# Sigmoid attention and a two-layer MLP: splitting of q, k, v and of the weights moved from GpSimd to ScalarE and VectorE

## Chip, cores and metric

The kernel runs on 1 core of one Trainium2 chip. The metric is the device time of one execution in microseconds (us).

## The reference

```python
scores = scale * np.matmul(q, k.transpose(0, 1, 3, 2)) - np.log(S)   # q, k, v: (8, 12, 448, 64) f32
attn = 1.0 / (1.0 + np.exp(-scores))
x = (attn @ v).transpose(0, 2, 1, 3).reshape(B * S, H * D)           # 3584 x 768
h = x @ w_in                                                         # w_in 768 x 2048
g = np.where(h >= 1, h, np.where(h <= -1, 0.0, (h + 1) ** 2 / 4))
out = g @ w_out                                                      # w_out 2048 x 768
```

## The kernel before

**Precision by splitting.** TensorE multiplies f16, and the kernel keeps f32 precision by writing a scaled operand as two f16 halves: hi is the f16 rounding of s*w, and lo is s*w - hi. A product then takes three matmuls (hi hi, hi lo, lo hi). What the change touches is who computes hi and lo. s is a power of two that is found from the largest magnitude.

**Attention.** Two heads form a pair; there are 48 pairs, six to a batch. Pairs 0 to 7 are multiplied as f32 from tensors that come laid out for it. Pairs 8 to 13 have q and k split (two parts of 128x448), pairs 14 to 47 have q, k and v split (two parts of 128x448 and one of 128x512). `load_pair` (L247) loads a pair three pairs ahead, `prep_a` (L267) finds the magnitudes on VectorE two pairs ahead, and `prep_b` (L283) finds the scales and splits. Then eight small DMAs on SyncE's queue copy the halves from `hl` into `qk` (L312, L313), and `scores`, `weigh` and `av` do the two products and the sigmoid, a piece (`step`) at a time. The raw tile has two buffers, so that a pair's load waits for the split of the pair two before.

In `prep_b` GpSimd does three instructions for each part: it scales the raw part in place (L303), writes hi (L304) and subtracts to get lo (L305).

**Weights.** w_in and w_out come as f64 words and are turned into f32 in 16 chunks each of 128x768 (`Weight.convert`: ScalarE L178 and L202, VectorE L185, L186 and L189). w_in's loads are on SyncE's queue during batch 0, w_out's mostly on ScalarE's. Once the scale of a group of eight chunks is known (`find_scale`), `Weight.split` writes the halves. It has two forms. With `pool` GpSimd scales in place (L220), ScalarE writes hi (L221), GpSimd writes lo (L222). Without it ScalarE writes hi with the scale (L224), and VectorE writes lo in one instruction (L225). Chunk f's halves lie where the f32 of chunk f-1 lay, so that the splits follow each other. Chunks 0 to 3 of w_in are split without `pool` (chunk 2 twice), 4 to 15 with it. In w_out every second chunk goes to GpSimd.

**MLP.** x of a batch is split (`finish_x`: ScalarE L448, VectorE L449). `up` makes 18 matmuls for a chunk (L517) and then g: ScalarE L526, VectorE L527 and L528, ScalarE L529 (hi), VectorE L530 (lo). L528 is the last reader of the PSUM tile `ph`, of whose tag there are three. `down` makes the second product (L549).

**Order.** Batch 0 is attention alone, together with the conversion of w_in. After it the units of the MLP of batch b are interleaved with the pieces of attention of batch b+1, and in batch 0's MLP with the rest of w_in, the conversion of w_out and its splits. Tile's scheduler orders every engine's instructions from the program order with priorities. Each engine then works its own list in order.

Of the kernel before, what the change touches and what calls it, by code (L numbers as in the profile page):

```python
# [18 lines left out]
AF = mybir.ActivationFunctionType  # L19
ALU = mybir.AluOpType  # L20
# [14 lines left out]
NHALF = 6  # L35

NA = 8
AHEAD = 2
LAST = 92
LAST1 = 20  # L40
# [4 lines left out]
B0 = 3  # L45
B1 = 64
GPOOL = 1
POOL_FROM = 2
MAX_ACT = 7
L0 = 10  # L50
A0 = 17
# [6 lines left out]
def sigmoid_attention_mlp(ctx: ExitStack, tc: tile.TileContext, first_qvk, qkv, w_in, w_out, out_t):  # L58
    nc = tc.nc
# [8 lines left out]
    NPIECE = NP * NPC  # L68
    GROUPS = slice(0, NA), slice(NA, NFC)
    LAG = 3  # L70
# [23 lines left out]
    def scales(m, n, tag, pool=None, square=False):  # L94

        pool = pool or sml_p
        few = {"bufs": 2} if tag == "x" else {}
        mask, top = (EXP_MASK - EXP_ONE, TOP - 1) if square else (EXP_MASK, TOP)
        e = sml_p.tile([P, 3], F32, tag="e", name=tag + "_e")[:, :n]
        nc.vector.tensor_scalar(out=e, in0=m, scalar1=TINY, scalar2=None, op0=ALU.max)  # L100
        ei = e.bitcast(I32)
        nc.vector.tensor_scalar(out=ei, in0=ei, scalar1=mask, scalar2=None, op0=ALU.bitwise_and)
        s = pool.tile([P, n], F32, tag=tag + "_s", name=tag + "_s", **few)
        nc.vector.tensor_scalar(  # L104
            out=s.bitcast(I32), in0=ei, scalar1=-1.0, scalar2=float((2 * 127 + top) * EXP_ONE), op0=ALU.mult, op1=ALU.add
        )
        inv = pool.tile([P, n], F32, tag=tag + "_i", name=tag + "_i", **few)
        nc.vector.tensor_scalar(  # L108
            out=inv.bitcast(I32), in0=ei, scalar1=float(top * EXP_ONE), scalar2=None, op0=ALU.subtract
        )  # L110
        return s, inv
# [7 lines left out]
        out=ident, in_=ident, pattern=[[-1, P]], compare_op=ALU.is_equal, fill=0.0, base=0, channel_multiplier=1  # L119
# [19 lines left out]
    class Weight:  # L139
# [27 lines left out]
        def convert(self):  # L167

            f = self.at - 2
            if 0 <= f < NFC:  # L170
                if f + 1 not in (NA, NFC):
                    self.sum(f)
                if self is wo:
                    self.load(3 if f == 3 else 1)
            f = self.at
            if f < NFC:
                a = self.f32(f)
                nc.scalar.activation(a, self.words_of(f)[1].bitcast(F32), AF.Abs, scale=HIGH_SCALE)  # L178
            f = self.at - 1
            if 0 <= f < NFC:  # L180

                low, high = self.words_of(f)
                a = self.f32(f)
                ai = a.bitcast(I32)
                nc.vector.tensor_scalar(out=ai, in0=ai, scalar1=3, scalar2=None, op0=ALU.logical_shift_left)  # L185
                nc.vector.scalar_tensor_tensor(  # L186
                    out=ai, in0=low, scalar=29, in1=ai, op0=ALU.logical_shift_right, op1=ALU.bitwise_or
                )
                nc.vector.scalar_tensor_tensor(  # L189
                    out=ai, in0=high, scalar=-0x80000000, in1=ai, op0=ALU.bitwise_and, op1=ALU.bitwise_or  # L190
                )
                if f + 1 in (NA, NFC):
                    self.sum(f)
                if self is wi:
                    self.load(1, nc.sync)
            self.at += 1
# [18 lines left out]
        def split(self, f, pool=False):  # L215
            if f >= NFC:
                return
            w, hi, lo, scale = self.f32(f), self.sb[:, f, 0, :], self.sb[:, f, 1, :], self.scale[f >= NA]
            if pool:
# [22 lines left out]
    def first_time(what, p):  # L242
        new = (what, p) not in done
        done.add((what, p))
        return new
# [37 lines left out]
    def prep_b(p):  # L283
        if not NFULL <= p < NPAIR or not first_time("split", p):
            return
        r, m = raws.pop(p), maxes.pop(p)
        n = 2 if p < NFULL + NHALF else 3

        s, inv = scales(m, n, "qkv")
        sqk = sml_p.tile([P, 1], F32, tag="sqk", name="sqk")  # L290
        nc.vector.tensor_scalar(
            out=sqk, in0=inv[:, 0:1], scalar1=inv[:, 1:2], scalar2=1.0 / math.sqrt(D), op0=ALU.mult, op1=ALU.mult
        )
        hl = hls.pop(p, None) or stk_p.tile([P, 2, 2, S], F16, tag="hl", name="hl")
        parts = [hl[:, 0], hl[:, 1]]
        if n == 3:
            v = stk_p.tile([P, 2, VW], F16, tag="v", name="v", bufs=3)
            parts.append(v)
        else:
            v = ready[p]  # L300
        for t, dst in enumerate(parts):
            rt, hi = r[:, t * S : 2 * S + VW if t == 2 else (t + 1) * S], dst[:, 0, :]
            nc.gpsimd.tensor_scalar(out=rt, in0=rt, scalar1=s[:, t : t + 1], scalar2=1.0, op0=ALU.mult, op1=ALU.mult)  # L303
            nc.gpsimd.tensor_scalar(out=hi, in0=rt, scalar1=1.0, scalar2=1.0, op0=ALU.mult, op1=ALU.mult)  # L304
            nc.gpsimd.tensor_tensor(out=dst[:, 1, :], in0=rt, in1=hi, op=ALU.subtract)  # L305

        qk = stk_p.tile([P, 2, 2, S], F16, tag="qk", name="qk")
        for j in range(2):
            src = slice(j * D, (j + 1) * D)
            for h in range(2):  # L310
                dst = slice(h * D, (h + 1) * D)
                nc.sync.dma_start(out=qk[dst, j, 0], in_=hl[src, 0, 0, :])  # L312
                nc.sync.dma_start(out=qk[dst, j, 1], in_=hl[src, 1, h, :])  # L313
        ready[p] = qk, v, sqk, inv, hl
# [168 lines left out]
    def group_scales(b, inv_x, k):  # L483

        up_sc[b, k] = sc = up_scales(*largest(inv_x, k), k)
        down_sc[b, k] = lambda: small("od%d" % k, inverse("ig%d" % k, sc[4]), wo.inv[k], ALU.mult)
# [24 lines left out]
    def up(b, f, u):  # L511
# [9 lines left out]
        if u == NCC // 2 - 1:  # L521
            ihr, hr, rt, ihs, _ = up_sc[b, int(f >= NA)]
            g = tmp_p.tile([P, S], F32, tag="tmp", name="g")
# [69 lines left out]
    wi = Weight(w_in, w_in_sb, "wi", [5 + 2 * (f % 6) for f in range(NFC)])  # L593
    wo = Weight(w_out, w_out_sb, "wo", [13, 15, 9, 11, 13, 15, 9, 11, 0, 0, 13, 15, 0, 0, 0, 0])
# [9 lines left out]
    with tc.manual_schedule(engines={mybir.EngineType.SP}):  # L604
# [9 lines left out]
        while at < NPIECE:  # L614
            step(at)
            at += 1
            for what, when in ((load_pair, L0), (prep_a, A0), (prep_b, A0 + 1)):
                for k in range(2):
                    if at == when + LSTEP * k:
                        what(NFULL + k)  # L620
            convert(wi, min((NA + 1) * at // WI_A, NA + 1 + max(0, at - WI_A) * (NFC - NA) // (NPIECE - WI_A + WI_B)))
            if at == WI_A:
# [11 lines left out]
    for u, unit in enumerate(units):  # L634
        while at < 2 * NPIECE and B0 + (at - NPIECE) * (B1 - B0) // NPIECE <= u:
            step(at)
            at += 1
        if wi.at < NFC + 1:
            n = NPIECE - WI_A
            convert(wi, NA + 1 + min(NFC - NA, (n + u + 1) * (NFC - NA) // (n + WI_B)))  # L640
            if wi.at == NFC + 1:
                wi.find_scale()
                group_scales(0, inv_x, 1)
        f, r = divmod(u, NCC // 2)
        if r == 0 and f < NFC:
            wi.split(f + AHEAD, f >= POOL_FROM)
        if wo.at < NA + 1:
            convert(wo, min(NA + 1, (u + 1) * (NA + 1) // WO_A))
            if wo.at == NA + 1:
                wo.find_scale()  # L650
                split_at = 0
        elif wo.at < NFC + 1:
            convert(wo, min(NFC + 1, NA + 1 + (u + 1 - WO_A) * (NFC - NA) // (WO_B - WO_A)))
            if wo.at == NFC + 1:
                wo.find_scale()
                roots()
        if len(wo.scale):
            while split_at < min(NA, 2 * (u + 1 - WO_A)):
                wo.split(split_at, split_at % 2 == 1)
                split_at += 1  # L660
        unit()
    inv_x = finish_x(1)
    common_scales(1, inv_x)
    for b in range(1, B):
        units = ups(b) + downs(b)
        last = LAST
        if b == 1:
            units = ups(1, 0, NA) + downs(0, 1) + ups(1, NA, NFC) + downs(1)
            last = len(units) - LAST1
        first = at  # L670
        for u, unit in enumerate(units):
            while at < min(b + 2, B) * NPIECE and (at - first) * (last - 1) // NPIECE <= u:
                step(at)
                at += 1
            if b == 1:
                while split_at < min(NFC, NA + (u + 1) * (NFC - NA) // (NA * NCC // 2 - 2)):
                    wo.split(split_at, split_at % 2 == 1)
                    split_at += 1
            unit()
            if b + 1 < B and u == last:  # L680
                inv_x = finish_x(b + 1)
                common_scales(b + 1, inv_x)
# [39 lines left out]
```

## Time and profile before

| | |
|---|---|
| median of 3 runs | 1202.59 us (1200.89 to 1203.66) |
| the profiled execution | 1202.2 us |
| its span, from the first to the last instruction | 1200.5 us |
| TensorE busy | 1166.8 us (97%) |
| VectorE, ScalarE, GpSimd busy | 64%, 47%, 31% of the span |
| mean granted TensorE clock | 0.994 |

A row of the profile names line, engine, operation and tiles (PE is TensorE, PEld its weight loads, DVE is VectorE, ACT ScalarE, POOL GpSimd, SPq SyncE's queue), output before input. Busy time is the time of the instructions; idle time is put down to what ended it.

### The profile page before, as it was taken

Reading aid. Unit: us, or ns where it says so; the run is one execution under the profiler, and the core shown is the slowest. Engines: PE = TensorE matmul, PEld = TensorE weight load, DVE = VectorE, ACT = ScalarE, POOL = GpSimd, SP = SyncE. Lnnn points to the kernel's source line nnn. Section 1 sums busy time; section 2 is a strip of 40 time slices with the busy share of each in tenths; the row PEclk is TensorE's granted clock in tenths of the full one; section 3 lists DMA queues with packets and bytes.
Section 4 is the critical chain, followed back from the end, with each engine's and each line's share of the span. In section 5 each row is a group of like instructions: output and inputs, shape, how many; then the busy total and the mean of one; then the engine's idle time right before and its main releaser. Section 6 shows DMA issues by size and latency. Waiting matters only on the chain.

```text
span 1200.5 us, 16814 instructions
## 1 busy us (share of the span) xinstructions
PE 1166.8 (97%) x6366; PEld 556.6 (46%) x6366; DVE 770.7 (64%) x1440; ACT 566.1 (47%) x811; POOL 371.4 (31%) x458
## 2 busy tenths in 40 slices
PE   7989799899999999999999999999999999999998
PEld 2324343444445444444444444454444444445554
DVE  6879978673753686458854787448874688336510
ACT  6979546452531554336533464336543466323300
POOL 0362665633420342413252234223424223100000
PEclk9999899999999999999999999999999999999999
DMA  9855125213120122212122112221212220100000
GB/s 320 316 191 210 49 57 180 88 40 117 54 82 24 48 56 64 73 58 75 40 71 79 56 40 55 87 56 50 77 41 75 63 68 17 31 22 10 1 16 31
DMA packets 47985, 92.72 MB, mean 77 GB/s; under 512 B 7712, under 2 KB 36896, under 8 KB 47904
## 3 DMA queue, kind: packets, MB, share of 16 engines
q1 hardware_dynamic: 46176, 82.21, 22.3%
q10 hardware_dynamic: 1728, 9.44, 2.2%
q8 instruction: 50, 0.82, 0.3%
q14 instruction: 31, 0.25, 0.1%
HBM read 60.88 MB, written 12.39 MB: 61 GB/s over the span
## 4 chain that ended last, share of the span: by engine, by line
PE 72%; issue 9%; DVE 7%; POOL 6%; DMA 3%; ACT 3%; SPq 0%; POOLq 0%; ACTq 0%; DVEq 0%
PE po L549 30%; PE ph L517 27%; PE pav L423 7%; PE psc L338 3%; PE psc L347 2%; PE psc L331 2%; POOL hl L305 1%; DMA raw<-qkv 1%; POOL raw L303 1%; POOL hl L304 1%; DMA w_out_sb<-w_in 1%; DVE m L280 1%; PE psc L353 1%; DVE g L527 1%; DVE w_out_sb L186 1%
## 5 line engine op out<-in xcount | busy, mean ns | idle before, releaser
L517 PE MATMUL ph<-xhl,w_in_sb 128*128 128x448 f16 x2304 | 449.1, 354 | 10.7 <-DVE g L528 6.1
L549 PE MATMUL po<-ghl,w_out_sb 128*128 128x448 f16 x2304 | 445.0, 353 | 0.9 <-DVE w_out_sb L225 0.9
L517 PEld LDWEIGHTS <-w_in_sb 128*128 128x128 f16 x2304 | 222.1, 98 | 237.2 <-issue 38.1
L549 PEld LDWEIGHTS <-w_out_sb 128*128 128x128 f16 x2304 | 221.8, 98 | 218.9 <-issue 13.7
L303 POOL TENSOR_SCALAR raw<-raw,qkv_s 128x448 f32<-128x448 f32 (+1 forms) x114 | 81.7, 731 | 527.2 <-DVE qkv_i L108 526.9
L382 ACT ACTIVATE psc<-psc,nls,sqk 128x896 f32<-128x896 f32 (+1 forms) x136 | 128.1, 972 | 212.9 <-PE psc L347 204.6
L391 DVE SCALAR_TENSOR_TENSOR ahl<-psc,ahl 128x896 f16<-128x896 f32 (+1 forms) x170 | 151.2, 900 | 68.1 <-ACT ahl L390 66.8
L390 ACT ACTIVATE ahl<-psc 128x896 f16<-128x896 f32 (+1 forms) x170 | 124.2, 763 | 51.2 <-DVE ahl L391 50.9
L529 ACT ACTIVATE ghl<-g 128x448 f16<-128x448 f32 x128 | 73.7, 577 | 123.8 <-DVE g L528 123.6
L280 DVE TENSOR_REDUCE m<-raw 128x2 f32<-128x896 f32 x74 | 63.5, 897 | 97.3 <-DMA raw<-qkv 97.3
L526 ACT ACTIVATE g<-ph,hr,ihr 128x448 f32<-128x448 f32 x128 | 92.2, 721 | 62.7 <-PE ph L517 55.2
L527 DVE SCALAR_TENSOR_TENSOR g<-g,rk 128x448 f32<-128x448 f32 x112 | 96.1, 858 | 21.2 <-ACT g L526 19.0
L530 DVE TENSOR_TENSOR ghl<-g,ghl 128x448 f16<-128x448 f32 x128 | 87.8, 686 | 34.0 <-ACT ghl L529 32.3
L305 POOL TENSOR_TENSOR hl<-raw,hl 128x448 f16<-128x448 f32 x80 | 92.5, 1175 | 0.0
L559 DVE TENSOR_SCALAR o<-po,od 128x448 f32<-128x448 f32 x48 | 32.6, 682 | 93.1 <-PE po L549 83.4
L528 DVE SCALAR_TENSOR_TENSOR g<-ph,ihs,g 128x448 f32<-128x448 f32 x128 | 87.2, 682 | 3.3
L423 PE MATMUL pav<-ahl,v 128*64 128x448 f16 x748 | 84.6, 356 | 0.0
L338 PE MATMUL psc<-qk 128*128 128x448 f16 x252 | 63.4, 354 | 1.5 <-ACT a L379 1.5
L331 PE MATMUL psc<-ghl 128*128 128x448 f32 (+1 forms) x128 | 51.4, 583 | 11.0 <-DMA ghl<-first_qvk 5.9
L448 ACT ACTIVATE xhl<-x,x_s 128x448 f16<-128x448 f32 x48 | 27.7, 655 | 69.6 <-DVE x_s L104 69.6
L423 PEld LDWEIGHTS <-v 128*64 128x64 f16 x748 | 38.8, 109 | 32.8 <-issue 12.6
L304 POOL TENSOR_SCALAR hl<-raw 128x448 f16<-128x448 f32 x80 | 52.8, 674 | 0.0
(114 smaller groups left out, 820.3 us busy)
## 6 DMA issues: line engine op xcount, KB each, us to landing
raw<-qkv SPq DMA_DIRECT2D x34, 704.0 KB, 4.3
qk<-hl SPq DMA_DIRECT2D x320, 56.0 KB, 2.0
w_out_sb<-w_in SPq DMA_DIRECT2D x16, 768.0 KB, 9.5
out_t<-o SPq DMA_DIRECT2D x48, 224.0 KB, 2.0
w_out_sb<-w_out ACTq DMA_DIRECT2D x6, 768.0 KB, 5.0
raww<-w_out ACTq DMA_DIRECT2D x6, 768.0 KB, 6.0
ghl<-first_qvk SPq DMA_DIRECT2D x8, 448.0 KB, 7.5
w_out_sb<-w_out SPq DMA_DIRECT2D x4, 768.0 KB, 8.0
```

Of the source, the lines that this page charges most:

```text
L303: nc.gpsimd.tensor_scalar(out=rt, in0=rt, scalar1=s[:, t : t + 1], scalar2=1.0, op0=ALU.mult, op1=ALU.mult)
L305: nc.gpsimd.tensor_tensor(out=dst[:, 1, :], in0=rt, in1=hi, op=ALU.subtract)
L338: nc.tensor.matmul(out, kq[:, j, 1, w], kq[:, j, 0, :], start=True, stop=False)
L382: nc.scalar.activation(a, a, AF.Sigmoid, bias=nls, scale=sqk)
L390: nc.scalar.activation(hi, x, AF.Copy, scale=ATT)
L391: nc.vector.scalar_tensor_tensor(out=lo, in0=x, scalar=ATT, in1=hi, op0=ALU.mult, op1=ALU.subtract)
L423: nc.tensor.matmul(pav[j * D : (j + 1) * D, :S], *terms[j][t], start=c == 0 and t == 0, stop=mid and t == len(terms[j]) - 1,)
L517: nc.tensor.matmul(ph[:, :S], w_in_sb[:, f, wh, c * P : (c + 1) * P], xhl[:, c, xh, :], start=c == 0 and wh + xh == 0, stop=c == NCC - 1 a ...
L526: nc.scalar.activation(g, ph[:, :S], AF.Relu, bias=hr, scale=ihr)
L527: nc.vector.scalar_tensor_tensor(out=g, in0=g, scalar=rt, in1=g, op0=ALU.min, op1=ALU.mult)
L530: (nc.gpsimd if f % GPOOL else nc.vector).tensor_tensor(out=ghl[:, f, 1, :], in0=g, in1=hi, op=ALU.subtract)
L549: nc.tensor.matmul(po[:, :S], w_out_sb[:, f, wh, m * P : (m + 1) * P], ghl[:, f, gh, :], start=f == lo and wh + gh == 0, stop=f == hi - 1 ...
```

## The change

Pairs 8 to 17 are now split as the weights already could be: ScalarE writes hi with the scale, VectorE writes lo in one instruction from the raw part and hi. Pairs 18 to 47 stay on GpSimd. All 16 chunks of w_out are split by ScalarE and VectorE. In w_in the odd chunks from 3 on go to GpSimd, the even ones to ScalarE and VectorE; chunk 3 thus moves to GpSimd, chunks 4, 6, 8, 10, 12 and 14 away from it.

```diff
+QK_POOL = 18
-POOL_FROM = 2
...
-            nc.gpsimd.tensor_scalar(out=rt, in0=rt, scalar1=s[:, t : t + 1], scalar2=1.0, op0=ALU.mult, op1=ALU.mult)
-            nc.gpsimd.tensor_scalar(out=hi, in0=rt, scalar1=1.0, scalar2=1.0, op0=ALU.mult, op1=ALU.mult)
-            nc.gpsimd.tensor_tensor(out=dst[:, 1, :], in0=rt, in1=hi, op=ALU.subtract)
+            st = s[:, t : t + 1]
+            if p < QK_POOL:
+                nc.scalar.activation(hi, rt, AF.Copy, scale=st)
+                nc.vector.scalar_tensor_tensor(
+                    out=dst[:, 1, :], in0=rt, scalar=st, in1=hi, op0=ALU.mult, op1=ALU.subtract
+                )
+            else:
+                nc.gpsimd.tensor_scalar(out=rt, in0=rt, scalar1=st, scalar2=1.0, op0=ALU.mult, op1=ALU.mult)
+                nc.gpsimd.tensor_scalar(out=hi, in0=rt, scalar1=1.0, scalar2=1.0, op0=ALU.mult, op1=ALU.mult)
+                nc.gpsimd.tensor_tensor(out=dst[:, 1, :], in0=rt, in1=hi, op=ALU.subtract)
...
-            wi.split(f + AHEAD, f >= POOL_FROM)
+            wi.split(f + AHEAD, f % 2 == 1)
...
-                wo.split(split_at, split_at % 2 == 1)
+                wo.split(split_at)
...
-                    wo.split(split_at, split_at % 2 == 1)
+                    wo.split(split_at)
```

## Rows read from the trace of the kernel before

**Rows 1.** Page, part 1: busy us, share of the span, instructions.

```profile
PE 1166.8 (97%) x6366; PEld 556.6 (46%) x6366; DVE 770.7 (64%) x1440; ACT 566.1 (47%) x811; POOL 371.4 (31%) x458
```

**Rows 2.** Waits of TensorE: total us, times, longest.

```profile
PE ph L517 <- DVE g L528: 6.1, 4, 2.0
...
PE pm L127 <- DVE g L528: 4.5, 2, 4.2
PE ph L517 <- ACT xhl L448: 3.1, 1, 3.1
...
PE psc L338 <- ACT a L379: 1.5, 1, 1.5
...
PE po L549 <- DVE w_out_sb L225: 0.9, 1, 0.9
```

**Rows 3.** Waits from 55 to 75 us, TensorE's on the sigmoid.

```profile
PE psc L331 <- ACT a L379: 3.5, 2, 2.0
```

**Rows 4.** Four stages: PE, PEld, DVE, ACT, POOL busy; granted clock, DMA.

```profile
40.00:75.00 35.00, 31.52 (x113) 10.66 (x111) 31.61 (x49) 29.03 (x45) 24.84 (x18) 0.99 0.58 189
75.00:120.00 45.00, 43.49 (x204) 17.22 (x202) 41.55 (x80) 40.05 (x63) 13.65 (x10) 0.97 0.66 249
120.00:165.00 45.00, 34.99 (x178) 16.07 (x175) 39.68 (x62) 25.05 (x41) 29.72 (x24) 0.92 0.20 58
165.00:255.00 90.00, 84.21 (x422) 35.77 (x420) 68.02 (x139) 48.82 (x69) 45.79 (x40) 0.98 0.32 96
```

**Rows 5.** VectorE's groups from 40 to 255 us: busy us, mean ns, idle before.

```profile
L530 DVE TENSOR_TENSOR ghl<-g,ghl 128x448 f16<-128x448 f32 x21 | 18.4, 874 | 7.0 <-ACT ghl L529 6.8
L527 DVE SCALAR_TENSOR_TENSOR g<-g,ru 128x448 f32<-128x448 f32 x16 | 16.8, 1052 | 1.2 <-ACT g L526 1.2
L528 DVE SCALAR_TENSOR_TENSOR g<-ph,ihs,g 128x448 f32<-128x448 f32 x21 | 14.2, 678 | 0.3
...
L225 DVE SCALAR_TENSOR_TENSOR w_out_sb<-w_out_sb,wo_s 128x768 f16<-128x768 f32 x8 | 10.5, 1314 | 5.0 <-ACT w_out_sb L224 4.8
...
L449 DVE SCALAR_TENSOR_TENSOR xhl<-x,x_s,xhl 128x448 f16<-128x448 f32 x12 | 9.6, 828 | 0.2 <-ACT xhl L448 0.2
```

**Rows 6.** VectorE's groups from 1040 to 1200 us, where GpSimd does nothing.

```profile
L527 DVE SCALAR_TENSOR_TENSOR g<-g,rk 128x448 f32<-128x448 f32 x16 | 11.0, 684 | 12.4 <-ACT g L526 12.4
L528 DVE SCALAR_TENSOR_TENSOR g<-ph,ihs,g 128x448 f32<-128x448 f32 x16 | 10.9, 684 | 0.5
L530 DVE TENSOR_TENSOR ghl<-g,ghl 128x448 f16<-128x448 f32 x16 | 10.0, 624 | 9.0 <-ACT ghl L529 9.0
...
L449 DVE SCALAR_TENSOR_TENSOR xhl<-x,x_s,xhl 128x448 f16<-128x448 f32 x6 | 4.0, 677 | 0.0
```

**Rows 7.** L225's instructions on w_out: ns min/median/max, first and last start.

```profile
L225 DVE SCALAR_TENSOR_TENSOR w_out_sb<-w_out_sb,wo_s x8: 1019/1188/1787, 173.3 to 238.6; 128x768 f16<-128x768 f32 x8
```

**Rows 8.** Stages of L527 alone: busy us and instructions.

```profile
120.00:165.00 45.00, 10.43 (x9) 0.92 0.20 58
```

**Rows 9.** Stages of L530 alone, the same columns.

```profile
120.00:165.00 45.00, 8.84 (x9) 0.92 0.20 58
```

**Rows 10.** GpSimd's groups from 40 to 255 us: busy us, mean ns, idle before.

```profile
L305 POOL TENSOR_TENSOR hl<-raw,hl 128x448 f16<-128x448 f32 x14 | 20.3, 1466 | 0.0
L303 POOL TENSOR_SCALAR raw<-raw,qkv_s 128x448 f32<-128x448 f32 x15 | 17.4, 1172 | 17.4 <-DVE qkv_i L108 17.1
...
L304 POOL TENSOR_SCALAR hl<-raw 128x448 f16<-128x448 f32 x14 | 11.6, 839 | 0.0
```

**Rows 11.** ScalarE's split of x from 40 to 255 us.

```profile
L448 ACT ACTIVATE xhl<-x,x_s 128x448 f16<-128x448 f32 x12 | 6.9, 657 | 0.0
```

**Rows 12.** Waits of SyncE's queue from 40 to 90 us.

```profile
SPq L312 <- POOL hl L304: 7.5, 1, 7.5
SPq L313 <- POOL hl L305: 5.2, 1, 5.2
```

**Rows 13.** Timeline of SyncE's queue: start us, us, issue.

```profile
74.07 0.52 SPq L159 DMA_DIRECT2D w_out_sb<-w_in  x1
```

## The prediction

> **What bounds the kernel now.** I read the busy times first. TensorE is busy for 1166.8 us of 1200.5 [rows 1], so that the whole of its idle time is 33.7 us, and nothing that other engines do is worth more than this and what a lowered clock costs. Then TensorE's waits, for whom the idle time is due [rows 2]: 6.1 and 4.5 us are waits for L528, VectorE's last read of `ph`, which frees the PSUM tile for the next chunk; 3.1 us is the first split of x; 1.5 us a late sigmoid and 0.9 us a late split of w_out. Another 3.5 us fall on two sigmoids at the end of batch 0 [rows 3]. Where they lie is seen in the busy times by stage [rows 4]: TensorE lacks 3.5, 1.5, 10.0 and 5.8 us in the stages up to 75, 120, 165 and 255 us, so that the stage from 120 to 165 holds nearly all of the waits for L528. In the same 45 us the granted clock is 0.92, so that a part of the stretch ran at 1.2 instead of 2.4 GHz. After 255 us TensorE hardly waits. So the question is what the change does to VectorE, ScalarE and SyncE's queue before 255 us. VectorE is the full one: 31.61 of 35, 41.55 of 45 and 39.68 of 45 us busy up to 165 us, then 68.02 of 90 [rows 4].
>
> **How much of VectorE's busy time is waiting for GpSimd.** The same instruction takes longer while GpSimd works. L527 takes 1052 ns on average and L530 874 ns before 255 us [rows 5], but 684 and 624 ns at the end, where GpSimd does nothing [rows 6]. L528, which reads PSUM for one of its inputs, takes 678 and 684 ns. So instructions with both inputs in SBUF are held up, and one with an input in PSUM isn't. What is lost in four groups: L527 16 x 0.368 = 5.9 us, L530 21 x 0.250 = 5.3, L449 12 x (0.828 - 0.677) = 1.8, and L225 on w_out 8 x (1.314 - 1.019) = 2.4 with the shortest as its own time [rows 5 to 7]. That is 15.4 us, a floor for 40 to 255 us, since the conversions of weights and the small scale computations aren't in it. These four groups are 55 of VectorE's 181 us there, and some of the rest, like L528, is immune; I take twice the floor, about 30 us, as an estimate of all.
>
> **What goes.** A part of q or k costs GpSimd 1.172 + 0.839 + 1.466 = 3.48 us there [rows 10]. 15 parts of pairs 8 to 14 are split before 255 us, 52 us. GpSimd is busy for 114.0 us in the four stages [rows 4]; the 62 us left are 20 chunks, 3.1 us each, of which 14 leave and one (chunk 3) comes, 40 us. So some 80% of GpSimd's work goes, and I take the same share of VectorE's loss: 12 us by the floor, 24 by the estimate.
>
> **What comes.** VectorE gets one instruction for a part, like L449: 0.677 us alone, 0.828 with what is lost to GpSimd now [rows 5, 6]. It gets 1.019 us, or 1.314, for a chunk [rows 5, 7]. Up to 165 us these are 8 parts (pairs 8 to 11) and five chunks net (4, 6, 8, 10, 12 and 14 less 3): 5.4 + 5.1 = 10.5 us alone, 13.2 at the longer times. From 165 to 255 us: 7 parts and 8 chunks of w_out, 13 us, for which VectorE has 22 us idle. Nine parts of pairs 15 to 17 come after 255 us, where TensorE doesn't wait; I cost them at nothing, and without that cover at 9 x 0.7 = 6 us. ScalarE gets 24 writes of 0.657 us [rows 11], eight of them before 165 us, 5.3 us beside 30 us that it has free there [rows 4]. In all VectorE's busy time stays about as it is: 24 us come and 12 to 24 go.
>
> At this place the Trainium skill speaks against the change: Perfetto Trace Analysis, section Optimizing Scalar/DVE Operations, says that GpSimd and VectorE share a read port, and that moving work between them might therefore not help. By that the sum would be zero, the rival "wash" below. The trace agrees as far as the sharing goes, with the 1052 against 684 ns of L527.
>
> **The terms**, against the profiled execution's 1202.2 us:
>
> 1. End of batch 0, the two sigmoids, 3.5 us [rows 3]. ScalarE is late there behind conversions, and these behind VectorE. SyncE's queue plays in: it waits 7.5 and 5.2 us for `hl` of GpSimd [rows 12], and a load of w_in stands behind the sixteen copies to `qk` until 74.07 us [rows 13], with the first loads of w_out behind it. When `hl` is written by two instructions a part instead of three long ones, these 12.7 us shrink, and the conversions get their data earlier. What it can give is 0 to 3.5 us, and 1.5 more in the next stage, which is all that TensorE lacks there. I take -3.5.
> 2. From 120 to 165 us, 10.6 us of waits for L528 [rows 2]. L527 and L530 lose 9 x (1.159 - 0.684) + 9 x (0.982 - 0.624) = 7.5 us there [rows 6, 8, 9]. Of GpSimd's 29.72 us four parts (13.9) and half of the chunk work (7.9) leave, 73%, so that 5.5 us come back; the added work is 4 x 0.677 + 4 x 1.019 = 6.8 us. By that sum alone nothing is gained. But what is lost now sits inside the chain from TensorE's result to L528, and the added instructions can stand beside it; and the earlier stages bring VectorE there with less left to do. Bounds: 0 and 10.6; I take -4, below the middle, since the sum speaks against more.
> 3. From 165 to 255 us, the late split of w_out and the late sigmoid, 0.9 + 1.5 us [rows 2]. With VectorE 22 us idle and no chunk of w_out going through GpSimd I take -2. The 3.1 us for x stay: this chain starts at the last piece of attention.
> 4. Clock: at 0.92 of 45 us at most 3.6 us are lost in stage three, partly while TensorE stands idle anyway. I take -1 with the shorter waits.
> 5. New waits: VectorE now waits in its order for ScalarE's hi, and g of the MLP is queued behind it, whose L528 TensorE waits for. The nearest rows: L449 waited 0.2 us in 12, L225 on w_out 4.8 us in 8 [rows 5]. For the 14 before 165 us that is 0.2 to 8.4 us. I take +2, nearer to L449, whose pattern the parts repeat.
>
> The sum is -8.5 us, so 1193.7; the profiled run is 0.4 us under the median of those shown, which makes 1194.0.
>
> **The rivals.** *Wash*: VectorE gets back what it is given, TensorE's waits stay and only change places: 1202, within 0.2%, which is 2.4 us and about what a measurement of this kernel can tell from no change. For it speaks the sum in term 2; against it the queue of term 1. *VectorE becomes the bound*: in the stages up to 165 us it has 12 of 125 us free, and the added lo has both inputs in SBUF, so that what GpSimd still does holds it up too. It decides when less than 10.5 us of loss come back there. If only the 5.5 us of term 2 come back, VectorE ends up 5.0 to 7.7 us longer, and TensorE waits for it: 1207 to 1210. For it speaks that VectorE is 88 to 92% busy in the three stages; against it that part of the busy time is loss. *All waits go*: 3.5 + 1.5 + 10.6 + 2.4 us and 2 us of clock, with no new waits: 20 us, 1182. Against it speaks term 5.
>
> **How the numbers follow.** I give the forecast (3 to 14 us faster) 0.52, all waits 0.11, wash 0.17, VectorE as the bound 0.20. The range reaches from 1184, near the end of "all waits", to 1205, between wash and the slower rival; some 0.06 lie below and 0.12 above. The likeliest case alone is 1188 to 1199. Of the wash a part ends just beyond 0.2% faster: 0.66 faster, 0.14 within 0.2%, 0.20 slower.
>
> **What would show it.** GpSimd's busy time falls from 371.4 to about 250 us, with no L222 on w_out and seven on w_in; L527's mean before 255 us falls towards 750 ns (term 2 and the estimate of the loss); SyncE's queue issues the load of 74.07 us some 6 us sooner and no longer waits 7.5 us for `hl` (term 1); TensorE's waits for L528 shrink below 7 us (term 2); VectorE's new instructions show idle time behind ScalarE of no more than 0.2 us each on average (term 5). The prediction is wrong if L527 gets shorter and TensorE's waits for L528 stay, or if those waits turn up behind the new lo instructions.

## Result, and the profile after

The changed kernel takes 1190.33 us (1188.77 to 1190.79, 4 runs) against 1202.01 us for the kernel before beside it: a ratio of 0.9899, 95% interval 0.9882 to 0.9917, 11.7 us faster. The forecast was 1194.0 us.

The page, part 1, of the changed kernel:

```profile
PE 1167.5 (98%) x6366; PEld 556.9 (47%) x6366; DVE 771.4 (65%) x1477; ACT 579.2 (49%) x835; POOL 263.3 (22%) x360
```

GpSimd gave up 108 us, VectorE's sum moved by 0.7 us, and TensorE's idle time fell from 33.7 to 21.2 us (against [rows 1]). TensorE's waits, total us, times, longest; the first is for the first load, which takes 5.9 us in the kernel before too:

```profile
PE psc L338 <- DMA ghl<-first_qvk: 6.5, 1, 6.5
PE psc L338 <- ACT a L386: 3.3, 2, 1.7
PE ph L524 <- ACT xhl L455: 2.6, 2, 1.3
PE psc L345 <- ACT a L386: 1.8, 2, 1.1
PE ph L524 <- DVE qkv_e L100: 1.5, 1, 1.5
PE ph L524 <- DVE xhl L456: 1.3, 2, 0.8
PE ph L524 <- DVE wo_e L102: 0.2, 1, 0.2
```

The lines after the change are numbered 7 higher: L535 is what L528 was, L534 is L527, L537 is L530. The waits of 6.1 and 4.5 us for the last read of `ph` [rows 2] are gone. The tiles `pm` of the small scale computations have the same PSUM tag as `ph`, and for VectorE's reads of one of these (L100) TensorE now waits 1.5 us. The split of x and the sigmoids are still waited for. By stage (PE, PEld, DVE, ACT, POOL busy with instructions, then clock and DMA):

```profile
40.00:75.00 35.00, 33.46 (x121) 11.54 (x121) 32.85 (x58) 33.29 (x52) 7.12 (x5) 1.00 0.80 273
75.00:120.00 45.00, 40.99 (x182) 15.70 (x182) 42.76 (x80) 39.41 (x65) 3.75 (x3) 0.92 0.59 209
120.00:165.00 45.00, 43.23 (x226) 20.17 (x223) 39.22 (x78) 28.84 (x46) 14.27 (x10) 1.00 0.19 51
165.00:255.00 90.00, 88.31 (x442) 37.90 (x440) 71.84 (x157) 59.28 (x86) 1.23 (x4) 0.98 0.33 101
```

Against [rows 4] TensorE is busy for 1.9 us more, 2.5 less, 8.2 more and 4.1 more. The counts say more than the busy times: from 40 to 165 us TensorE has done 529 matmuls instead of 495, and VectorE 216 instructions instead of 191, in 114.8 us of busy time instead of 112.8. So a VectorE instruction took 532 ns on average instead of 591, with 13 new ones among them by the prediction's count; the mix of long and short ones differs too, so this mean alone shows little. Its groups from 40 to 255 us (busy us, mean ns, idle before) show which got shorter:

```profile
L225 DVE SCALAR_TENSOR_TENSOR w_out_sb<-w_out_sb,wo_s 128x768 f16<-128x768 f32 x16 | 16.3, 1018 | 3.2 <-ACT w_out_sb L224 3.1
L535 DVE SCALAR_TENSOR_TENSOR g<-ph,ihs,g 128x448 f32<-128x448 f32 x23 | 15.5, 680 | 0.2
L537 DVE TENSOR_TENSOR ghl<-g,ghl 128x448 f16<-128x448 f32 x23 | 15.4, 675 | 4.5 <-ACT ghl L536 4.4
L534 DVE SCALAR_TENSOR_TENSOR g<-g,ru 128x448 f32<-128x448 f32 x16 | 11.4, 712 | 0.0
...
L306 DVE SCALAR_TENSOR_TENSOR hl<-raw,qkv_s,hl 128x448 f16<-128x448 f32 x16 | 10.5, 680 | 0.0
```

Against [rows 5] L527 went from 1052 to 712 ns, L530 from 874 to 675, L225 on w_out from 1314 to 1018, and L528, with an input in PSUM, stayed (678 and 680). The new instruction L306 takes 680 ns and never waited for ScalarE. Over all groups that both kernels have in this stretch, the smaller count of the two times the difference of the means adds up to 25 us, 12.6 of them up to 165 us: so much less do the same VectorE instructions take.

### The profile page after: what moved, and what is told of

It reads as the page before. It is cut to its first block, busy times and chain, and to the rows that moved or that the text cites. A ratio compares the mean times of both kernels' runs of the same rounds, so it can differ in the third digit from the quotient of the medians.

```text
span 1188.7 us, 16763 instructions
## 1 busy us (share of the span) xinstructions
PE 1167.5 (98%) x6366; PEld 556.9 (47%) x6366; DVE 771.4 (65%) x1477; ACT 579.2 (49%) x835; POOL 263.3 (22%) x360
## 4 chain that ended last, share of the span: by engine, by line
PE 90%; DVE 4%; ACT 2%; DMA 1%; SPq 1%; issue 1%; POOL 0%; ACTq 0%; DVEq 0%
PE po L556 37%; PE ph L524 34%; PE pav L430 9%; PE psc L345 4%; PE psc L354 3%; PE psc L338 2%; PE psc L360 1%; ACT a L386 1%; DVE w_out_sb L186 1%; DMA raw<-qkv 1%; DMA w_out_sb<-w_in 1%; DVE w_out_sb L189 1%; PE psc L340 1%; DVE ghl L537 0%; DVE g L534 0%
## 5 line engine op out<-in xcount | busy, mean ns | idle before, releaser
L310 POOL TENSOR_SCALAR raw<-raw,qkv_s 128x448 f32<-128x448 f32 (+1 forms) x90 | 58.2, 661 | 485.8 <-DVE qkv_i L108 465.2
L534 DVE SCALAR_TENSOR_TENSOR g<-g,rk 128x448 f32<-128x448 f32 x112 | 94.9, 848 | 21.5 <-ACT g L533 19.2
L537 DVE TENSOR_TENSOR ghl<-g,ghl 128x448 f16<-128x448 f32 x128 | 83.7, 656 | 29.3 <-ACT ghl L536 27.6
L535 DVE SCALAR_TENSOR_TENSOR g<-ph,ihs,g 128x448 f32<-128x448 f32 x128 | 87.1, 682 | 3.2
L312 POOL TENSOR_TENSOR hl<-raw,hl 128x448 f16<-128x448 f32 x60 | 66.5, 1127 | 0.0
L430 PEld LDWEIGHTS <-v 128*64 128x64 f16 x748 | 38.7, 109 | 32.3 <-issue 12.6
L371 POOL COPY w_in_sb<-hl 64x64 f16<-64x64 f16 x68 | 20.3, 298 | 138.8 <-ACT hl L305 118.4
```

Source lines behind the costliest of these rows:

```text
L430: nc.tensor.matmul(pav[j * D : (j + 1) * D, :S], *terms[j][t], start=c == 0 and t == 0, stop=mid and t == len(terms[j]) - 1,)
L534: nc.vector.scalar_tensor_tensor(out=g, in0=g, scalar=rt, in1=g, op0=ALU.min, op1=ALU.mult)
L535: nc.vector.scalar_tensor_tensor(out=g, in0=ph[:, :S], scalar=ihs, in1=g, op0=ALU.mult, op1=ALU.max)
L537: (nc.gpsimd if f % GPOOL else nc.vector).tensor_tensor(out=ghl[:, f, 1, :], in0=g, in1=hi, op=ALU.subtract)
```

## Experiments

Each time is a median beside runs of the kernel before (1202 us); the ratio is to those. The scheduler writes new lists for the engines with nearly every edit, so that a run shows the edit together with its new order, except for one pair below.

**The parts alone.** Only q, k, v; only w_in; only w_out. The edits are the three places of the change, put back in turn:

```diff
 # qkv_only, win_only and wout_only keep one of these three each
-QK_POOL = 18
+QK_POOL = 0
-            wi.split(f + AHEAD, f % 2 == 1)
+            wi.split(f + AHEAD, f >= 2)
-                wo.split(split_at)
+                wo.split(split_at, split_at % 2 == 1)
```

> Only q, k and v of pairs 8 to 17 move to ScalarE and VectorE; the weights are split as before. Theory LOCK (GpSimd's reads of SBUF hold up VectorE's instructions on the chain from TensorE's result to its last read of ph, and their going is the gain): of the GpSimd work that the change takes out of the stage from 120 to 165 us, 13.9 of 21.8 us are these parts, so 6 to 7 us faster than before (about 1195.5), with TensorE's waits for the last read of ph down from 10.6 to some 4 us. Rival QUEUE (the copies to qk no longer hold up SyncE's queue, weights come earlier, and all follows from that): the whole gain or nearly, 1191. Rival CHAIN (ScalarE no longer waits for GpSimd between two chunks): little, 1200 to 1202.

Measured: 1190.75 us, 0.9901 (0.9886 to 0.9915), 11.2 us faster.

> Only w_in's chunks change (the odd ones from 3 on to GpSimd, the even ones to ScalarE and VectorE); q, k, v and w_out as before. LOCK: half of the chunk work leaves the stage from 120 to 165 us, 7.9 of 21.8 us, so 3 to 4 us faster (about 1198.5). QUEUE: nothing, 1202. CHAIN: the waits of ScalarE for GpSimd in this stage (5.1 us) go, 5 to 6 us faster, 1196.

Measured: 1202.84 us, 1.0000 (0.9990 to 1.0009), no change.

> Only w_out's chunks change (all to ScalarE and VectorE); q, k, v and w_in as before. They are split after 172 us, where VectorE has 22 us idle. LOCK: 0.9 and 1.5 us of waits go there, 2 us faster, 1200. QUEUE: nothing, 1202. CHAIN: 10.4 us of waits of ScalarE for GpSimd go, 4 us faster, 1198.

Measured: 1197.81 us, 0.9966 (0.9956 to 0.9976), 4.2 us faster.

The parts of q, k and v alone give what the whole change gives. LOCK missed all three numbers. The run on w_in does not try CHAIN, since ScalarE's waits for GpSimd didn't go in it (from 120 to 165 us: the kernel before, w_in only, q, k, v only):

```profile
ACT w_in_sb L221 <- POOL w_in_sb L222: 5.1, 3, 3.0
ACT w_in_sb L224 <- POOL w_in_sb L222: 7.7, 2, 6.5
ACT w_in_sb L221 <- POOL w_in_sb L222: 6.5, 3, 5.2
```

What speaks against CHAIN as the cause of the whole is the third row: q, k and v gave all of the gain while ScalarE waited longer in this stage. In the run on w_out, where waits of 10.4 us went, CHAIN's number came true (1198). At this point QUEUE looked best.

**Pairs 8 and 9.** First the changed kernel with these two back on GpSimd (`if 10 <= p < QK_POOL:`), then the kernel before with these two alone moved (`QK_POOL = 10`, the weights as before).

> The changed kernel, with pairs 8 and 9 back on GpSimd. LOCK: their 16 us of GpSimd work lie before 75 us, where TensorE waits only 3.5 us, and the stage from 120 to 165 us stays free of waits for the last read of ph; 0 to 3 us slower than the changed kernel, 1190 to 1193. QUEUE: SyncE's queue issues the load of w_in at about 74 us again instead of 67, most of the gain is lost, 1198 or more. In both the split of x of batch 0 may come sooner, since fewer conversions of w_out have their data by then.

Measured: 1199.19 us, 0.9973 (0.9961 to 0.9984), 8.9 us slower than the changed kernel. LOCK had the stage from 120 to 165 us free of waits for the last read of `ph`; they came back, though nothing of these two pairs is split there:

```profile
PE ph L524 <- DVE g L535: 5.4, 2, 3.4
```

> The kernel before with nothing changed but pairs 8 and 9: their four parts of q and k are split by ScalarE and VectorE. QUEUE (the copies to qk of these two pairs hold up the loads behind them on SyncE's queue; conversions of w_out come later and crowd the stage from 120 to 165 us): 8 to 10 us faster, 1192 to 1194, with the first nine chunks of w_out converted by about 125 us instead of 138. LOCK (GpSimd's reads hold up VectorE): these parts are 16 us of GpSimd's 114 before 255 us and none of them after 75 us, so 1 to 2 us faster, 1200 to 1201.

Measured: 1196.40 us, 0.9951 (0.9937 to 0.9965), 5.7 us faster, between the two expectations. That leaves 5.5 us of the run on q, k and v for pairs 10 to 17, but the run before gained only 2.8 us without pairs 8 and 9, so the two shares don't simply add up. Its stages:

```profile
40.00:75.00 35.00, 33.40 (x121) 11.21 (x119) 31.49 (x57) 33.04 (x51) 8.25 (x6) 1.00 0.73 246
75.00:120.00 45.00, 41.94 (x188) 16.58 (x187) 44.75 (x83) 40.97 (x66) 14.68 (x9) 0.92 0.60 215
120.00:165.00 45.00, 39.15 (x197) 17.63 (x195) 37.03 (x59) 24.08 (x40) 30.45 (x25) 0.96 0.17 43
165.00:255.00 90.00, 88.08 (x435) 36.17 (x433) 67.83 (x141) 51.00 (x73) 47.52 (x43) 0.98 0.30 95
```

Where the two pairs are split TensorE gains 1.9 us of busy time and gives 1.5 back in the next stage; 4.2 us come from 120 to 165 us and 3.9 after that, where nothing of them is left. (This execution took 1198.0 us; its TensorE was busy for 1171.0 us in all, 4.2 more than before, so that these sums are more than the time that it gained.) From 40 to 75 us VectorE has done 57 instructions instead of 49 [rows 4], four of them new, so that four others were out of the way later.

**The queue.** Two edits take QUEUE apart. In the kernel before, the copies of pairs 8 and 9 leave SyncE's queue; in the changed kernel they stand on it twice.

```diff
 # before_copies_pool, on the kernel before
-                nc.sync.dma_start(out=qk[dst, j, 0], in_=hl[src, 0, 0, :])
-                nc.sync.dma_start(out=qk[dst, j, 1], in_=hl[src, 1, h, :])
+                q = nc.gpsimd if p < 10 else nc.sync
+                q.dma_start(out=qk[dst, j, 0], in_=hl[src, 0, 0, :])
+                q.dma_start(out=qk[dst, j, 1], in_=hl[src, 1, h, :])
...
 # after_copies_twice, on the changed kernel; the loops stand inside it
+        for _ in range(2 if p < 10 else 1):
```

> The kernel before with all splits as they were; only the sixteen copies to qk of pairs 8 and 9 are issued on GpSimd's queue instead of SyncE's. QUEUE: SyncE's queue is free for the load of w_in before 70 us, and the gain comes without any split moved: 5 to 9 us faster, 1193 to 1197 (GpSimd has the issuing to do). LOCK: the same reads of SBUF by GpSimd, so no gain, 1201 to 1203.

Measured: 1204.81 us, 1.0021 (1.0011 to 1.0030), 2.7 us slower. Its SyncE queue (start us, us, issue) did what was wanted, the load of w_in at 51 us instead of 74.07 [rows 13]:

```profile
51.02 0.85 SPq L159 DMA_DIRECT2D w_out_sb<-w_in  x2
```

> The changed kernel with the sixteen copies to qk of pairs 8 and 9 issued twice, the second time with the same data. That is 16 more issues of 0.6 us ahead of the load of w_in on SyncE's queue, about 9 us, and hardly any work for an engine. QUEUE: the load goes out at about 76 us, and most of the gain is lost, 1196 to 1200. LOCK: as the changed kernel, 1190 to 1191.

Measured: 1188.73 us, 0.9892 (0.9878 to 0.9906). The load went out at 77.41 us, later than in the kernel before, and all of the gain stayed:

```profile
77.41 0.58 SPq L159 DMA_DIRECT2D w_out_sb<-w_in  x1
```

So an early load brought nothing and a late one took nothing: QUEUE falls. The first of the two runs alone would leave a doubt, as GpSimd had the issuing to do; the second has no such cost.

**Reads against writes.** The changed kernel with idle work for GpSimd beside each part that it no longer splits. Nobody waits for its result. The two kernels' lists of VectorE, ScalarE, TensorE and SyncE are the same instruction for instruction; they differ only in what GpSimd does.

```diff
 # both
-    out_p = ctx.enter_context(tc.tile_pool(name="outp", bufs=2))
+    out_p = ctx.enter_context(tc.tile_pool(name="outp", bufs=1))
 # decoy_read, for each part of pairs 8 to 17
+                for _ in range(2):
+                    nc.gpsimd.tensor_scalar(out=dy, in0=dx, scalar1=st, scalar2=1.0, op0=ALU.mult, op1=ALU.mult)
+                    nc.gpsimd.tensor_scalar(out=dy, in0=dx, scalar1=1.0, scalar2=1.0, op0=ALU.mult, op1=ALU.mult)
+                    nc.gpsimd.tensor_tensor(out=dy, in0=dx, in1=dx, op=ALU.subtract)
 # decoy_write
+                nc.gpsimd.tensor_scalar(out=dy[:, :1], in0=dx[:, :1], scalar1=st, scalar2=1.0, op0=ALU.mult, op1=ALU.mult)
+                for _ in range(7):
+                    nc.gpsimd.memset(dy, 1.0)
```

> The changed kernel with idle work for GpSimd: beside each part of q, k and v of pairs 8 to 17 that ScalarE and VectorE split, GpSimd does six instructions that read a 128x224 tile of SBUF which nothing else uses, some 2 us a part, released by the same scale as the old split. Nothing waits for their result; the output tile has one buffer instead of two to make room. LOCK: VectorE's instructions with two inputs in SBUF get longer again, and some of the gain is lost: 3 to 8 us slower than the companion kernel with writes alone. If the reads don't matter (theory ORDER: the gain comes from which engine waits for whom, above all ScalarE for GpSimd), both take the same time within 2 us.

Measured: 1201.26 us, 0.9991 (0.9981 to 1.0001): the gain is gone. A part took GpSimd 4.5 us and not 2.

> The companion: the same places, but after one instruction on a single column GpSimd only writes the tile, seven times, and reads nothing. VectorE, ScalarE, TensorE and SyncE have instruction for instruction the same lists as in the kernel with reads. LOCK: near the changed kernel, 1189 to 1192, and 3 to 8 us faster than with reads. ORDER: the same time as with reads.

Measured: 1194.56 us, 0.9934 (0.9922 to 0.9947), 6.7 us faster than with reads, and the intervals are far apart. It is also 4.2 us slower than the changed kernel, above the range that LOCK gave; that part is not due to reads of the tile, and stays unexplained. The profiled executions took 1201.3 and 1191.4 us, the second being the fastest of its five, and their spans 1199.5 and 1189.7 us, so that the rows below show 9.8 us of difference. The stages with reads:

```profile
40.00:75.00 35.00, 29.30 (x103) 9.97 (x101) 28.46 (x50) 26.81 (x43) 23.37 (x27) 1.00 0.76 266
75.00:120.00 45.00, 39.85 (x166) 14.73 (x167) 42.19 (x72) 39.53 (x64) 5.69 (x3) 0.89 0.53 189
120.00:165.00 45.00, 42.87 (x227) 20.10 (x227) 43.29 (x80) 31.08 (x50) 30.31 (x32) 1.00 0.18 54
```

And with writes:

```profile
40.00:75.00 35.00, 32.80 (x118) 11.22 (x117) 30.57 (x57) 32.29 (x50) 17.96 (x37) 1.00 0.77 271
75.00:120.00 45.00, 40.40 (x186) 15.67 (x187) 43.69 (x81) 40.25 (x66) 4.67 (x3) 0.96 0.58 207
120.00:165.00 45.00, 42.96 (x225) 20.12 (x222) 39.82 (x79) 28.68 (x46) 24.01 (x42) 1.00 0.17 47
```

From 40 to 165 us VectorE gets through 202 instructions of its list with reads and 217 with writes, and TensorE through 496 and 529 matmuls. These are the figures of the kernels before and after the change: 191 and 216 (of other lists), 495 and 529. But LOCK, as it was put, is only half of it. From 40 to 255 us L527's counterpart took 841 ns with reads and 792 with writes, a small difference; matched one by one, VectorE's 366 instructions that start in this stretch with writes take 218.3 us with reads and 208.2 with writes, 10.2 us in all. The waits for the last read of `ph` did not come back with the reads:

```profile
PE ph L531 <- DVE g L542: 0.4, 1, 0.4
```

The other half is that GpSimd's own reads are held up as well. Its timeline shows it, since VectorE stood idle from 68.8 to 75.1 us (start us, us):

```profile
65.49 1.42 POOL L313 TENSOR_SCALAR dy<-dx,qkv_s 128x224 f16<-128x224 f32 x1
67.00 0.95 POOL L314 TENSOR_SCALAR dy<-dx 128x224 f16<-128x224 f32 x1
68.04 1.14 POOL L315 TENSOR_TENSOR dy<-dx 128x224 f16<-128x224 f32 x1
69.28 0.45 POOL L313 TENSOR_SCALAR dy<-dx,qkv_s 128x224 f16<-128x224 f32 x1
69.82 0.38 POOL L314 TENSOR_SCALAR dy<-dx 128x224 f16<-128x224 f32 x1
70.28 0.56 POOL L315 TENSOR_TENSOR dy<-dx 128x224 f16<-128x224 f32 x1
```

Its groups from 40 to 255 us (busy us, mean ns):

```profile
L315 POOL TENSOR_TENSOR dy<-dx 128x224 f16<-128x224 f32 x30 | 24.5, 817 | 2.5
L313 POOL TENSOR_SCALAR dy<-dx,qkv_s 128x224 f16<-128x224 f32 x31 | 22.8, 737 | 59.9 <-DVE qkv_i L108 57.5
L314 POOL TENSOR_SCALAR dy<-dx 128x224 f16<-128x224 f32 x30 | 20.3, 678 | 2.4
```

These are 67.6 us where the writes and their single-column reads took 46.0. Behind them on GpSimd's list stood its lo of chunk 3, for which ScalarE waited, and for ScalarE's sigmoid TensorE (waits from 55 to 82 us, with reads):

```profile
PE psc L345 <- ACT a L393: 7.5, 2, 6.0
...
ACT w_in_sb L227 <- POOL w_in_sb L225: 6.0, 1, 6.0
```

With writes ScalarE waited 1.1 us and TensorE 1.9 us there. Of the 9.8 us between the two profiled executions 4.9 have arisen by 75 us, where the same VectorE instruction ends that much later with reads; the rest comes bit by bit up to 255 us.

**Chunk 3.** The same chain stands in the run with pairs 8 and 9 back on GpSimd. Its ScalarE waited 5.25 us (timeline of ScalarE, idle before in brackets):

```profile
71.61 0.93 ACT L224 ACTIVATE w_in_sb<-w_in_sb,wi_s 128x768 f16<-128x768 f32 x1 [5.25 <-POOL w_in_sb L222]
```

The edit is `wi.split(f + AHEAD, f % 2 == 1 and f > 1)` on top of that run's.

> Pairs 8 and 9 back on GpSimd, as in an earlier run, but with chunk 3 of w_in on ScalarE and VectorE, as it was before the change. ORDER: in that earlier run ScalarE waited 5.2 us for GpSimd's lo of chunk 3, which stood behind the 16 us of splits of pairs 8 and 9, and TensorE 4.4 us for the sigmoid behind that; this wait goes, and the kernel is 3 to 5 us faster than that run, 1194 to 1196. LOCK alone: the reads are the same to within one chunk, 1198 to 1199.

Measured: 1198.26 us, 0.9968 (0.9955 to 0.9980), no different from that run (0.9973): LOCK's number, not ORDER's. The wait went, and others came:

```profile
PE psc L338 <- ACT a L386: 6.7, 4, 2.2
...
PE ph L524 <- DVE qkv_e L100: 4.6, 1, 4.6
```

So ORDER's single wait was not what the run lost; where it was taken away, VectorE and ScalarE were late elsewhere.

**How the parts combine.** q, k, v and w_out without w_in (`f >= 2` back), and the change with all of w_in on ScalarE and VectorE (`wi.split(f + AHEAD)`).

> The change without its part on w_in: q, k, v and w_out moved, w_in split as before. If the parts add up, 11.2 + 4.2 us faster than before, 1187; if the two gains are the same waits of TensorE, as the whole change gains no more than q, k, v alone, 1190 to 1191.

Measured: 1192.75 us, 0.9921 (0.9907 to 0.9934), 9.4 us faster: w_out adds nothing to q, k, v. The traces fit that. Alone, w_out gains 3.7 us of TensorE's time from 165 to 255 us, where its chunks are split (first row, against 84.21 us in [rows 4]); with q, k and v alone TensorE stands idle no more in this stage (second row), so nothing was left there to gain.

```profile
165.00:255.00 90.00, 87.89 (x440) 37.07 (x438) 70.86 (x149) 53.52 (x74) 28.89 (x30) 1.00 0.32 96
165.00:255.00 90.00, 90.00 (x444) 37.81 (x443) 74.16 (x154) 56.76 (x81) 24.66 (x20) 1.00 0.33 103
```

> The changed kernel with the odd chunks of w_in on ScalarE and VectorE too, so that GpSimd splits no weight and nothing before pair 18. LOCK: the last 12 us of GpSimd's reads from 120 to 165 us go, 1 to 2 us faster than the changed kernel, 1188 to 1189. QUEUE: no difference from the queue; VectorE gets 7 us more where it is 87 to 95% busy, 0 to 3 us slower, 1190 to 1193.

Measured: 1192.30 us, 0.9918 (0.9905 to 0.9932), 9.8 us faster; the last reads of GpSimd gave nothing when they went, with more work for VectorE in exchange. No version was faster than the changed kernel beyond the intervals.

## Why the prediction was right

Direction and size held, the measured 11.7 us against the 8.6 forecast, and so did the cause that was named, GpSimd's work beside a full VectorE: some 25 us of VectorE's instructions came back before 255 us, against an estimate of 24. That the sum came so near is in part luck, as its errors cancel: by TensorE's busy time in the stages term 1 came out at +0.6 us instead of -3.5, terms 2 and 3 at twice their size, and the +2 of term 5 stayed away. (The sum itself is 1194.1 and not 1194.0, 0.4 us being added to 1193.7.) The terms one by one:

1. *End of batch 0* (-3.5): failed. SyncE's queue did move as forecast, the load of w_in at 66.70 us and 4.9 us as its longest wait for `hl`, but the two runs on the queue show that this is worth nothing. TensorE's first waits shrank by 1.9 us, yet its first matmul on the split x came later, at 88.20 instead of 85.75 us, and the next stage lost 2.5. The scale of x is found by small instructions on VectorE. In the kernel before (timeline of VectorE) they follow each other:

```profile
81.82 0.30 DVE L136 TENSOR_REDUCE xm<-pm 128x1 f32<-128x128 f32 x1
...
82.53 0.15 DVE L104 TENSOR_SCALAR x_s<-x_e 128x1 int32<-128x1 int32 x1
```

and after the change:

```profile
79.80 0.28 DVE L136 TENSOR_REDUCE xm<-pm 128x1 f32<-128x128 f32 x1
...
82.80 0.15 DVE L100 TENSOR_SCALAR x_e<-xm 128x1 f32<-128x1 f32 x1
...
85.68 0.14 DVE L102 TENSOR_SCALAR x_e<-x_e 128x1 int32<-128x1 int32 x1
...
86.61 0.14 DVE L104 TENSOR_SCALAR x_s<-x_e 128x1 int32<-128x1 int32 x1
```

6.8 us instead of 0.7, since VectorE's list now has longer instructions between them, conversions of w_out above all. TensorE then ran the first chunk at a granted clock of 0.75 from 90 to 100 us: 18 matmuls in 5.85 us, which took 3.56 before.

2. *From 120 to 165 us* (-4): right in where the gain lies, and half as large as measured. The waits for L528 went from 10.6 us to nothing, TensorE gained 8.2 us of busy time, and the clock of the stage rose from 0.92 to 1.00. What was mis-sized: I set the added 6.8 us against 5.5 us that come back in the same stage. The run with pairs 8 and 9 alone shows that relief in an earlier stage reaches this one, 4.2 us of it. That these waits end because L527 and L530 get shorter in this stage, as the term has it, is not shown: the run with pairs 8 and 9 back has 5.4 us of them and no more work for GpSimd there than the changed kernel (13.1 against 14.3 us, where it was 29.7), the run with reads has 0.4 us of them with GpSimd 30.3 us busy. Nor do they go with the time: with the copies on GpSimd's queue there were 2.4 us of them at 1204.81 us, with the copies twice 4.5 at 1188.73. What comes late on VectorE and ScalarE shows now at one wait, now at another.

3. *From 165 to 255 us* (-2): 4.1 us. The late split of w_out and the late sigmoid are gone, and the wait at the split of x, which I had kept, shrank from 3.1 to 1.3 us. (It stands at 228 us in the kernel before and is for x of the second batch; the prediction's first paragraph calls it the first.)

4. *Clock* (-1): nothing in sum. The stage from 120 to 165 us gained what the one before it lost (0.97 to 0.92).

5. *New waits* (+2): did not come. L306 waited 0.0 us in 16; L225 on w_out 3.1 us in 16, where VectorE has room.

The rule of the Trainium skill (Perfetto Trace Analysis, section Optimizing Scalar/DVE Operations) that moving work between GpSimd and VectorE might not help did not come true here: VectorE's sum stayed, as by the rule, and the kernel got faster. Nearer is SBUF — State Buffer, section Who interferes with whom: a VectorE instruction with two inputs in SBUF contends with a GpSimd instruction that reads SBUF, and not with one that only writes it. The pair of runs agrees: 6.7 us between reads and writes, with the same lists elsewhere.

The rival of the slower side, VectorE as the bound, was set to decide below 10.5 us of relief up to 165 us. The relief was larger, 12.6 us by the groups that both kernels have, and 25 more instructions, 13 of them new by the prediction's count, cost VectorE only 2.0 us of busy time there.

What stays open: how much of the gain is VectorE held up by GpSimd, and how much GpSimd held up by VectorE with ScalarE waiting for it. The pair of runs gives 6.7 us for both together, and the one with chunk 3 shows that it can't be told by taking one wait away. Open too are the 4.2 us between the kernel with writes and the changed kernel.

## What to carry to other kernels

When two engines hold each other up, compare their instructions' means in a stretch where one of them is idle, and count the instructions that get done, not the busy time: here VectorE's busy time stayed while it did 25 instructions more in the same 125 us. A gain from a relieved engine comes out where the bound engine waits, which can be two stages later, so cost it over the whole stretch in which that engine is full. And an early load or a single visible wait is worth what an experiment on it alone shows: both that looked decisive here were worth nothing.

## Not expected of the hardware

Four parts of q and k, 16 us of GpSimd's work before 75 us, cost 5.7 to 8.9 us at the end, although TensorE waits only 3.5 us in that stretch [rows 3]. And an instruction of GpSimd on a single column, among its writes, took 511 ns on average (18 of them, 9.2 us from 40 to 255 us).
